# Two weight loads in one transfer each, their remainders ahead, and a bias in four transfers

## The chip, the cores and the metric

The kernel runs on one core of one Trainium2 chip. The time is the device time of an execution in microseconds (us); a median is given with its number of runs. The profiles come from single executions. Their span is from the first to the last instruction of the core, about 1.8 us shorter than the time. Ratios are computed as the mean time of one kernel's fast runs over that of the other's of the same rounds, so they are not quite the ratio of the medians quoted.

## The reference

Two tokens pass through a layer norm; then an attention over the last 2,048 keys of a cache and a squared-ReLU MLP run side by side, and both are added to the input.

```
q   = xn @ wq                          # wq: 576 x 4096
o   = softmax(q k^T / sqrt(128)) v     # 16 KV heads, 32 query heads
h   = relu(xn @ w1 + b1) ** 2          # w1: 576 x 4608
out = x + o @ wo + (h @ w2 + b2)
```

Keys, values and weights are 53 MB of bfloat16 that have to be loaded once. There is next to no arithmetic per byte.

## The kernel before

Keys and values come in 16 transfers of 2 MB (one 16,384 B row per partition) into six buffers. A packet is what one of the 16 DMA engines moves at once; in the records of this kernel that is one row of a partition, or a write of 4 B that tells a semaphore that an engine's share has landed. A semaphore is a counter on which an instruction can wait. wq and w1 have 576 = 4 x 128 + 64 rows. The first 512 come in two transfers, two rows to a partition each; the last 64, the remainder, in a third behind them:

```python
wbig = ctx.enter_context(tc.tile_pool(name="wbig", bufs=NFULL // RW))   # NFULL = 4, RW = 2
...
if i < NFULL // RW:
    tl = wbig.tile([P, RW * WBW], BF16, tag="wbig", name=f"{name}_{i}")
    rows = wt[0:NFULL * P, :].rearrange("(p r) n -> p (r n)", r=NFULL)
    nc.sync.dma_start(out=tl[:, 0:RW * width], in_=rows[:, i * RW * width:(i + 1) * RW * width])
    ...
else:
    tl = wrem.tile([P, WRW], BF16, tag="wrem", name=f"{name}_rem")
    nc.sync.dma_start(out=tl[:, 0:lrem], in_=wt[NFULL * P:D, :].rearrange("r (s l) -> (r s) l", s=S))
```

The large loads are issued on SP (SyncE), the small ones (input, biases, a few w2 rows) on ACT (ScalarE). All of them take eight semaphores in turn: a load waits until the one eight before it has landed. That is not written in the kernel. It is in the built program, and it changes whenever a load is added or removed. The matmuls of q use the four large rows first and the remainder last, and those of the MLP do the same with w1. The last w2 rows reuse w1's buffer.

## Time and profile before

| | before |
|---|---|
| time, median | 134.68 us (3 runs, 134.59 to 134.82) |
| span | 132.8 us |
| TensorE, VectorE, ScalarE busy | 66%, 43%, 35% |
| loads busy, slices 2 to 38 of 40 | 90% or more |
| packets of the SP loads | 4,320 |

How to read it: no compute engine is near its limit, and the DMA engines are busy from the first load to the last. The prediction below shows the lines and works from them. A queue's line holds packets, MB and share of the 16 engines' span. A line of the timeline holds start and length in us, engine (SPq is SP's own sequence of issues), line of the program, operation, and tile <- source; in brackets stand the idle time of the engine before it and what ended it.

### The profile page before, as it was taken

The page shows a single profiled execution, that of the slowest core. Times are in us where ns is not written, and L with a number is a line of the kernel's source. Part 1 is how long each engine was busy: PE and PEld are TensorE (multiplying, and loading weights), DVE is VectorE, ACT ScalarE, POOL GpSimd, SP SyncE. Part 2 cuts the span into 40 slices and gives each one's busy share as a digit, 9 for nine tenths or more (in the row PEclk, how much of TensorE's full clock was granted, in tenths as well). Part 3 has the DMA queues.
Part 4 walks back from the last instruction along what each step waited for, and adds up shares of the span by engine and source line. Part 5 has one row for each costly group of instructions (what it writes and reads, how often), then busy time and mean ns, then how long its engine had stood idle before and what let it go on. Part 6 is the DMA issues. An engine that isn't in the chain of part 4 may idle for free.

```text
span 132.8 us, 2335 instructions
## 1 busy us (share of the span) xinstructions
PE 87.0 (66%) x982; PEld 53.4 (40%) x982; DVE 57.4 (43%) x156; ACT 46.8 (35%) x64; POOL 5.2 (4%) x17
## 2 busy tenths in 40 slices
PE   0069737997678597397496499779725495647261
PEld 0058414375335354264264346536412154137150
DVE  7724404235465466366377437457520424350000
ACT  5715503167383276265265244366120400000000
POOL 6000000010100000100100100010100000000000
PEclk9999995559999999999999757999985555555955
DMA  4999999999999999999999999999999999999960
GB/s 124 423 414 439 419 432 434 429 424 436 410 454 423 439 419 426 422 424 434 422 434 429 429 434 442 429 433 416 433 417 440 434 421 433 427 413 431 405 239 1
DMA packets 4507, 53.76 MB, mean 405 GB/s; under 512 B 535, under 2 KB 762, under 8 KB 1278
## 3 DMA queue, kind: packets, MB, share of 16 engines
q1 hardware_dynamic: 4320, 53.32, 94.7%
q10 hardware_dynamic: 178, 0.31, 0.6%
q8 instruction: 7, 0.11, 0.3%
q14 instruction: 2, 0.02, 0.0%
HBM read 53.62 MB, written 0.00 MB: 404 GB/s over the span
## 4 chain that ended last, share of the span: by engine, by line
DMA 77%; PE 13%; SPq 4%; DVE 2%; issue 1%; ACT 0%; DVEq 0%
DMA w_rem<-in_B_w_dram 28%; DMA w<-in_B_w_dram 20%; DMA k<-in_A_k_cache_dram 17%; DMA wq_rem<-in_A_wq_dram 13%; PE kT_ps L109 8%; PE sc_ps L106 3%; SPq L134 2%; DVE qrow L292 1%; SPq L127 1%; PE o_ps L106 1%; PE qT_ps L109 1%; DVE kT L328 1%; PE out_ps L106 1%; DVE qz L308 0%; SPq L158 0%
## 5 line engine op out<-in xcount | busy, mean ns | idle before, releaser
L109 PE MATMUL kT_ps<-ident_f,k 128*128 128x128 f32 x256 | 41.9, 311 | 11.5 <-DMA k<-in_A_k_cache_dram 8.2
L109 PEld LDWEIGHTS kT_ps<-ident_f,k 128*128 128x128 f32 x256 | 32.5, 159 | 26.1 <-issue 13.2
L326 ACT COPY kT<-kT_ps 128x1024 bf16<-128x1024 bf16 x32 | 31.9, 1013 | 19.4 <-PE kT_ps L109 19.3
L328 DVE COPY kT<-kT_ps 128x1024 bf16<-128x1024 bf16 x32 | 21.8, 682 | 15.2 <-PE kT_ps L109 15.0
L106 PE MATMUL sc_ps<-kT,qz 128*32 128x512 bf16 x128 | 10.5, 413 | 5.8 <-DVE kT L328 5.8
L358 ACT ACTIVATE p<-sc_ps,bias 128x512 bf16<-128x512 f32 x8 | 5.5, 687 | 20.2 <-DVE gown L354 20.2
L106 PE MATMUL o_ps<-v,pT 128*32 128x512 bf16 x128 | 12.1, 475 | 0.0
L572 ACT CAST fin_sb<-out_ps 113x144 bf16<-113x144 f32 x1 | 0.3, 278 | 24.6 <-PE out_ps L106 24.6
L347 DVE TENSOR_REDUCE m<-sc_ps 128x1 f32<-128x512 f32 x8 | 5.5, 691 | 7.2 <-PE sc_ps L106 7.2
L387 DVE SCALAR_TENSOR_TENSOR o<-o_ps,in_s,o 128x128 f32<-128x128 f32 x24 | 8.3, 346 | 0.5
L361 DVE STREAM_TRANSPOSE pT<-p 128x512 bf16<-128x512 bf16 x8 | 5.7, 710 | 6.5 <-ACT p L358 6.5
L106 PE MATMUL out_ps<-w,hT_sb 128*17 128x144 bf16 x136 | 4.6, 295 | 4.4 <-DMA w<-in_B_w_dram 4.2
L385 DVE TENSOR_SCALAR o<-o_ps,in_s 128x128 f32<-128x128 f32 x8 | 2.7, 343 | 9.6 <-PE o_ps L106 9.6
L106 PEld LDWEIGHTS <-hT_sb 128*17 128x17 bf16 (+2 forms) x172 | 4.6, 117 | 5.7 <-issue 5.7
L106 PEld LDWEIGHTS <-xnT 128*2 128x2 bf16 x100 | 2.4, 94 | 10.8 <-issue 9.7
L351 POOL PARTITION_ALL_REDUCE gmax<-m x8 | 2.9, 365 | 90.3 <-DVE m L349 90.3
L106 PEld LDWEIGHTS <-qz 128*32 128x32 bf16 x128 | 2.2, 98 | 10.0 <-DVE kT L328 7.4
L106 PE MATMUL op_ps<-o,of_h 128*128 128x129 f32 x16 | 4.0, 334 | 3.2 <-DVE o L387 3.2
L106 PE MATMUL h_ps<-w,xnT 128*2 128x384 bf16 x48 | 3.2, 422 | 4.1 <-DMA w<-in_B_w_dram 4.1
L109 PE MATMUL pro_ps<-ident,tmp_x 2*128 2x2 bf16 x6 | 0.5, 175 | 6.6 <-DVE tmp_x L232 6.6
L106 PEld LDWEIGHTS op_ps<-o,of_h 128*128 128x128 f32 x16 | 2.8, 220 | 5.0 <-DVE o L387 5.0
L452 DVE TENSOR_TENSOR hrow<-t 98x384 bf16<-98x384 f32 x3 | 1.6, 556 | 6.5 <-ACT t L451 6.3
(74 smaller groups left out, 55.1 us busy)
## 6 DMA issues: line engine op xcount, KB each, us to landing
k<-in_A_k_cache_dram SPq DMA_DIRECT2D x8, 2048.0 KB, 12.0
v<-in_A_v_cache_dram SPq DMA_DIRECT2D x8, 2048.0 KB, 23.7
wo<-in_A_wo_dram SPq DMA_DIRECT2D x2, 2304.0 KB, 27.4
w<-in_B_w_dram SPq DMA_DIRECT2D x2, 2304.0 KB
wq<-in_A_wq_dram SPq DMA_DIRECT2D x2, 2048.0 KB, 16.6
w<-in_B_w_dram SPq DMA_DIRECT2D x3, 1296.0 KB, 27.6
w_rem<-in_B_w_dram SPq DMA_DIRECT2D x1, 576.0 KB
w<-in_B_w_dram SPq DMA_DIRECT2D x1, 576.0 KB
```

The lines of the kernel that those rows point to most:

```text
L106: tc.keep_in_program_order(nc.tensor.matmul(*a, **k))
L109: tc.keep_in_program_order(nc.tensor.transpose(*a, **k))
L134: nc.sync.dma_start(out=tl[:, 0:RW * width], in_=rows[:, i * RW * width:(i + 1) * RW * width])
L326: nc.scalar.copy(out=kT, in_=kT_ps[:])
L328: nc.vector.tensor_copy(out=kT, in_=kT_ps[:])
L347: nc.vector.tensor_reduce(out=m1[:], in_=sc_ps[:], axis=AX.X, op=ALU.max)
L351: nc.gpsimd.partition_all_reduce(gmax[:], m2[:], channels=P, reduce_op=ReduceOp.max)
L358: nc.scalar.activation(out=p_sb[:], in_=sc_ps[:], func=ACT.Exp, bias=bias[:, 0:1], scale=scale, accum_out=o1[:, Dh:Dh + 1])
L361: nc.vector.transpose(out=pT[:].rearrange("p j r -> p (j r)"), in_=p_sb[:])
L385: nc.vector.tensor_scalar(scalar1=in_s[:, 0:1], scalar2=None, op0=ALU.mult, **kw)
L387: nc.vector.scalar_tensor_tensor(scalar=in_s[:, k:k + 1], in1=o1[:, 0:Dh], op0=ALU.mult, op1=ALU.add, **kw)
L452: nc.vector.tensor_tensor(out=hrow[:, k * HB:(k + 1) * HB], in0=t1, in1=t1, op=ALU.mult)
```

## The change

The intent is fewer and larger packets: four rows of a partition in one piece (32,768 B for wq, 36,864 B for w1), with the small remainder ahead. The first MLP bias goes the other way, from one transfer of four rows to four transfers of one row.

```diff
-    wbig = ctx.enter_context(tc.tile_pool(name="wbig", bufs=NFULL // RW))
+    wbig = ctx.enter_context(tc.tile_pool(name="wbig", bufs=1))
...
-        if i < NFULL // RW:
-            tl = wbig.tile([P, RW * WBW], BF16, tag="wbig", name=f"{name}_{i}")
-            rows = wt[0:NFULL * P, :].rearrange("(p r) n -> p (r n)", r=NFULL)
-            nc.sync.dma_start(out=tl[:, 0:RW * width], in_=rows[:, i * RW * width:(i + 1) * RW * width])
+        if i == 1:
+            tl = wbig.tile([P, NFULL * WBW], BF16, tag="wbig", name=f"{name}_big")
+            nc.sync.dma_start(out=tl[:, 0:NFULL * width],
+                              in_=wt[0:NFULL * P, :].rearrange("(p r) n -> p (r n)", r=NFULL))
...
-    NW = NFULL // RW + 1
+    NW = 2
...
-    nc.scalar.dma_start(out=b1_sb[:], in_=B_b1.rearrange("(g n) -> g n", g=NG4))
+    b1_rows = B_b1.rearrange("(g n) -> g n", g=NG4)
+    for i in range(0, NG4, NG4 // 4):
+        nc.scalar.dma_start(out=b1_sb[i:i + NG4 // 4, :], in_=b1_rows[i:i + NG4 // 4, :])
```

## The prediction

> **What bounds the kernel now.** I read the slices of the span first, because a kernel that loads 53 MB for two tokens is likely to be bound by its loads, then the DMA queues, then the chain of waits, and last the issues and the matmuls around the two weight loads that change. Slices, queues and the chain's shares by engine, from the page of the kernel before:
>
> ```profile
> DMA  4999999999999999999999999999999999999960
> GB/s 124 423 414 439 419 432 434 429 424 436 410 454 423 439 419 426 422 424 434 422 434 429 429 434 442 429 433 416 433 417 440 434 421 433 427 413 431 405 239 1
> ...
> q1 hardware_dynamic: 4320, 53.32, 94.7%
> q10 hardware_dynamic: 178, 0.31, 0.6%
> q8 instruction: 7, 0.11, 0.3%
> ...
> DMA 77%; PE 13%; SPq 4%; DVE 2%; issue 1%; ACT 0%; DVEq 0%
> ```
>
> The 16 DMA engines are 90% busy or more in every slice of 3.32 us but the first and the last two, at 405 to 454 GB/s. 94.7% + 0.6% + 0.3% of 132.8 us is 126.9 us, and from the first load packet (2.2 us) to the last (129.2 us) there are 127.0 us. So there is no hole to fill. The packet records say it more sharply: on the engine that finishes first, the completions of consecutive 2 MB transfers lie at 28.19, 33.06, 37.92 and 42.78 us, 4.86 us apart. That is 131,072 B per engine in 4.86 us, 27.0 GB/s, times 16 engines 431 GB/s.
>
> The end of the chain, in order of time (start, length, what):
>
> ```profile
> 65.68 36.87 DMA w_rem<-in_B_w_dram
> 102.55 0.02 issue
> 102.56 26.58 DMA w<-in_B_w_dram
> 129.14 0.04 issue
> 129.18 0.69 PE out_ps L106 x10
> 129.88 0.02 issue
> 129.90 0.28 ACT fin_sb L572
> ```
>
> The last w2 rows land, ten matmuls, one cast, then the output store: 3.6 us of tail after the last byte. The piece "w_rem 36.87" is not a slow transfer, it is one that stood in line. The end is therefore: start of the loads + bytes over rate + tail.
>
> **What the Trainium skill says.** All three places are in the page "DMA: Bandwidth & Descriptors". Section "Where 436 GB/s comes from" gives the ceiling of the 16 ports as 435 GB/s; the trace agrees, 431 GB/s steady. Section "Why small descriptors are slow (HBM only)" names a fixed cost of about 3 cycles per packet. The records agree that it is small: consecutive packets of one engine start 47 ns apart at 1,152 B, 89 at 2,304 B, 174 at 4,608 B, 607 at 16,384 B and 682 at 18,432 B. A line of 0.0367 ns per byte plus 5 ns fits all five. Section "Why a DMA increments its semaphore by 16 and not by 1" says that the number of engines is the largest factor up to 16 of the slowest dimension, taken from the lowest-numbered engine. The trace agrees: the bias load of 4 rows left four packets of 2,304 B, at 17.90 to 17.95 us, each with one semaphore write; a load of one row leaves one.
>
> **The change part by part.**
>
> *Packets.* 4,320 packets on the load queue are 3,840 rows and 30 transfers x 16 semaphore writes. One row of a partition is one packet up to 18,432 B, the largest here. The change makes wq 128 packets of 32,768 B instead of 256 of 16,384 B, and w1 128 of 36,864 B instead of 256 of 18,432 B; the bytes stay. That removes 16 row packets and 2 semaphore writes per engine, about 5 ns each: 18 x 5 = 0.09 us. By the line a packet takes 1,208 and 1,358 ns; that it holds beyond 18,432 B is an estimate of mine. If the hardware splits such rows, the gain is 0.
>
> *First bias.* Four loads of one row instead of one of four put all four packets on the lowest engine: 3 x (89 + 6) = 0.28 us more there, 0.1 us less on the next three. The engines do not end together: their last w2 packets end at 126.81, 127.05, 127.06 and 127.33 us on four of them and between 128.17 and 129.21 us on the other twelve; the last decides. Following completions from transfer to transfer (5 engines carry the 5-partition w2 remainders, 2 the input rows, 1 the second bias), I find the lowest engine ending near 128.4 us and the slowest as one of the next three; where two completions lie within 10 ns this following is uncertain. So the added 0.28 us ends at 128.7 us, hidden, and the slowest may gain 0.1 us. Issuing four instead of one costs ACT 3 x 0.26 us near 14.3 us, where it idles until 20.95 us.
>
> *wq in one piece.* The matmuls of q as they stand:
>
> ```profile
> 14.86 1.03 PE L106 MATMUL q_ps<-wq,xnT 128*2 128x512 bf16 x16
> 18.66 1.03 PE L106 MATMUL q_ps<-wq,xnT 128*2 128x512 bf16 x16 [2.77 <-DMA wq<-in_A_wq_dram]
> 19.91 0.99 PE L106 MATMUL q_ps<-wq_rem,xnT 128*2 128x512 bf16 x8 [0.21 <-DMA wq_rem<-in_A_wq_dram]
> ```
>
> The same bytes have landed at about 19.9 us in either order, but then 40 matmuls remain instead of 8: 2 x 1.03 = 2.1 us later for q, for the first scores and for the k buffers that they free. Does that starve the loads? The issue of k after the second unit's transposes stands at 33.62 us and its bytes move only from 50.4 us; 2.1 us out of 16.8. TensorE then waits for k at 35.57, 45.60 and 55.86 us (0.41, 0.61 and 2.17 us), which swallows the delay by the fifth unit.
>
> *Waits of the issuing queue.* The two builds differ in which earlier load each issue waits for, because the loads take eight semaphores in turn and the number of loads changes. The issues of before:
>
> ```profile
> 8.43 0.55 SPq L127 DMA_DIRECT2D k<-in_A_k_cache_dram  x1
> 9.02 0.60 SPq L127 DMA_DIRECT2D v<-in_A_v_cache_dram  x1
> 10.96 0.54 SPq L127 DMA_DIRECT2D k<-in_A_k_cache_dram  x1
> 18.64 0.53 SPq L127 DMA_DIRECT2D v<-in_A_v_cache_dram  x1
> ```
>
> After it, the second k waits for the wq remainder (about 9.4 us), and the first v for the whole of wq (about 19.5 us); the next ones follow at once. While v waits, one k transfer (4.86 us) is still to move. Issue to first packet took 1.5 us at the start (0.72 to 2.19 us); the engines' spread at that point is 0.9 us. 4.86 - 0.9 - 1.5 leaves 2.5 us: no hole, but it is the thinnest place. ACT's own bias loads wait for the first k (landed 8.1 us) and for w2 pieces, all done by 14 us.
>
> *w1 in one piece.* The MLP and the last matmuls:
>
> ```profile
> 95.98 1.15 PE L106 MATMUL h_ps<-w,xnT 128*2 128x384 bf16 x24
> 101.21 2.09 PE L106 MATMUL h_ps<-w,xnT 128*2 128x384 bf16 x24 [4.08 <-DMA w<-in_B_w_dram]
> 103.09 1.18 PE L106 MATMUL h_ps<-w_rem,xnT 128*2 128x384 bf16 x12
> ...
> 120.88 1.29 PE L106 MATMUL out_ps<-w,hT_sb 128*17 128x144 bf16 x36
> 123.98 0.74 PE L106 MATMUL out_ps<-w,hT_sb 128*17 128x144 bf16 x36 [1.81 <-DMA w<-in_B_w_dram]
> 127.08 2.77 PE L106 MATMUL out_ps<-w,hT_sb 128*17 128x144 bf16 x64 [2.37 <-DMA w<-in_B_w_dram]
> ```
>
> All 60 matmuls now start at about 102.3 us. At the slow rate of the second line (2.09 us for 24) they take 5.2 us and end at 107.5 us instead of 104.3: up to 3.2 us later. Behind them TensorE has 1.81 + 2.37 = 4.2 us of waiting for w2 before the last piece, so the delay dies there with 1 us to spare. The last w2 pieces reuse w1's buffer, now one buffer, so their issue moves from the first half's matmuls to behind all of the large w1 part: about 107 us, while their bytes move from 123 us on.
>
> *Sum.* -0.09 us for packets, 0 to -0.1 us for the bias, 0 for the order: 134.68 - 0.15, about 134.5 us.
>
> **Rivals.** (1) The lowest engine is the slowest after all: +0.28 - 0.09 us, 134.9 us; for it speaks only the uncertain following of engines. (2) The MLP's delay exceeds the 4.2 us, because the granted clock falls further there: each us beyond adds 1 us, 135 to 136 us; against it, the estimate already uses the slow rate. (3) A hole at the first v: up to 1 us, 135.5 us. (4) Large packets run at another rate: the two loads take 20 of the 127 us, so 5% either way is 1 us; nothing in the line bends at 18,432 B. (5) The 7 instruction fetches of 16 KB (about 0.95 us each) fall on other engines; the slowest engine moves by some tenths either way.
>
> **Range and chances.** The sum and rivals 1 and 5 lie within 0.5 us; 134.0 to 135.0 us holds most of it. A change by 2% is 2.7 us: it needs rival 2 or 4 at a size nothing suggests.
>
> **What would show it.** Load packets fall from 4,320 to 4,320 - 256 - 32 = 4,032. The DMA slices stay at 9 and the last w2 lands at 129.0 us within 0.5. The q matmuls all stand after 19 us, the MLP's after 102 us, and the waits for w2 shrink from 4.2 us to about 1 us without vanishing. I am wrong if a slice shows under 9 before the end, if the last output matmuls no longer wait for w2, or if the large packets leave the line.

## The result, and the profile after

The changed kernel takes 134.47 us (median of 6 fast runs, 134.31 to 134.48); the kernel before took 134.63 us in its 6 runs by then (134.57 to 134.82). The ratio is 0.9984, with a 95% interval of 0.9971 to 0.9997: the same at 2%, and 0.16 us faster by the medians. The interval leaves a gain between 0.04 and 0.39 us.

Slices and queues, from the page of the changed kernel:

```profile
DMA  4999999999999999999999999999999999999960
GB/s 139 409 415 488 425 397 416 430 430 415 444 418 431 433 420 427 431 430 430 418 440 420 440 430 432 421 457 432 478 405 388 425 425 450 407 423 428 416 247 1
...
q1 hardware_dynamic: 4032, 53.32, 94.6%
q10 hardware_dynamic: 178, 0.31, 0.6%
```

The row of nines is unbroken, and the packets fell by 288 to the predicted 4,032. The single slices of 488 and 388 GB/s are no change of speed: a packet is now up to 1.36 us long and is counted in one of the 3.3 us slices. For the same reason a second profile of the same kernel shows one slice of 8 near 100 us, although by its packet records no engine stood idle there. The issues on SP at the start, from the timeline:

```profile
9.50 0.55 SPq L126 DMA_DIRECT2D k<-in_A_k_cache_dram  x1
19.80 0.54 SPq L126 DMA_DIRECT2D v<-in_A_v_cache_dram  x1
20.38 0.60 SPq L126 DMA_DIRECT2D k<-in_A_k_cache_dram  x1
```

SP now stands still from 10.1 to 19.8 us, until the large wq load has landed. No slice shows a hole, because the k transfer issued at 9.50 us was still in line. The matmuls of q:

```profile
19.82 3.58 PE L105 MATMUL q_ps<-wq_big,xnT 128*2 128x512 bf16 x32 [5.02 <-DMA wq_big<-in_A_wq_dram]
23.19 0.87 PE L105 MATMUL q_ps<-wq_rem,xnT 128*2 128x512 bf16 x8
```

q is done at 24.06 us instead of 20.90, 3.2 us later; by 56 us, where TensorE waits 1.68 us for k, it is back where it was (56.06 against 55.86 us). The MLP and the last matmuls:

```profile
102.52 3.64 PE L105 MATMUL h_ps<-w_big,xnT 128*2 128x384 bf16 x48 [7.89 <-DMA w_big<-in_B_w_dram]
105.98 0.66 PE L105 MATMUL h_ps<-w_rem,xnT 128*2 128x384 bf16 x12
...
123.57 2.37 PE L105 MATMUL out_ps<-w,hT_sb 128*17 128x144 bf16 x72
127.00 0.74 PE L105 MATMUL out_ps<-w,hT_sb 128*17 128x144 bf16 x36 [1.06 <-DMA w<-in_B_w_dram]
128.39 0.43 PE L105 MATMUL out_ps<-w,hT_sb 128*17 128x144 bf16 x16 [0.65 <-DMA w<-in_B_w_dram]
129.10 0.66 PE L105 MATMUL out_ps<-w,hT_sb 128*17 128x144 bf16 x12 [0.28 <-DMA w<-in_B_w_dram]
```

The MLP ends at 106.64 us instead of 104.27, and the waits for w2, 1.81 + 2.37 us before, are now 1.06 + 0.65 + 0.28 = 2.0 us. They shrank but did not vanish: the loads still set the end. By the packet records the last load ends at 129.13 us against 129.21.

Where do the 0.16 us come from? The profiled spans differ by 0.17 us (132.81 and 132.64 us). 0.08 us of it is the last packet's end. The rest lies behind it, and 0.07 us of that was in nobody's sum: from the landing of the output store to the end of the program it is 1.24 us before and 1.17 us after. In the built program SP closes with five instructions that each wait for a pair of the semaphores, in a fixed order; each costs about 60 ns (53 to 70 ns by the table in the experiments). The store's semaphore is in the fourth of them before, so one more follows after it has landed. The change adds one load in sum, the turn moves on by one, and the store's semaphore falls into the fifth, the last one.

### The profile page after: what moved, and what is told of

It reads as the page before. It is cut to its first block, busy times and chain, and to the rows that moved or that the text cites. A ratio compares the mean times of both kernels' runs of the same rounds, so it can differ in the third digit from the quotient of the medians.

```text
span 132.6 us, 2337 instructions
## 1 busy us (share of the span) xinstructions
PE 84.1 (63%) x982; PEld 52.2 (39%) x982; DVE 57.2 (43%) x156; ACT 46.7 (35%) x64; POOL 5.2 (4%) x17
## 2 busy tenths in 40 slices
DMA packets 4219, 53.76 MB, mean 405 GB/s; under 512 B 503, under 2 KB 730, under 8 KB 1246
## 3 DMA queue, kind: packets, MB, share of 16 engines
q1 hardware_dynamic: 4032, 53.32, 94.6%
## 4 chain that ended last, share of the span: by engine, by line
DMA 62%; PE 4%; DVE 1%; ACT 1%; issue 1%; ACTq 0%
DMA v<-in_A_v_cache_dram 29%; DMA w<-in_B_w_dram 17%; DMA k<-in_A_k_cache_dram 16%; PE kT_ps L108 3%; PE o_ps L105 1%; ACT kT L325 1%; PE sc_ps L105 1%; ACT p L357 1%; DVE pT L360 1%; DVE kT L327 0%; DVE o L386 0%; PE out_ps L105 0%; ACT fin_sb L573 0%; DVE o L384 0%; PE op_ps L105 0%
## 5 line engine op out<-in xcount | busy, mean ns | idle before, releaser
L108 PE MATMUL kT_ps<-ident_f,k 128*128 128x128 f32 x256 | 40.0, 303 | 9.3 <-DMA k<-in_A_k_cache_dram 7.0
L108 PEld LDWEIGHTS kT_ps<-ident_f,k 128*128 128x128 f32 x256 | 31.5, 155 | 22.6 <-issue 11.6
L105 PE MATMUL o_ps<-v,pT 128*32 128x512 bf16 x128 | 11.6, 461 | 0.0
L105 PEld LDWEIGHTS <-xnT 128*2 128x2 bf16 x100 | 3.1, 112 | 17.7 <-issue 17.5
L105 PE MATMUL h_ps<-w_big,xnT 128*2 128x384 bf16 x48 | 3.6, 484 | 7.9 <-DMA w_big<-in_B_w_dram 7.9
L105 PE MATMUL q_ps<-wq_big,xnT 128*2 128x512 bf16 x32 | 3.6, 625 | 5.0 <-DMA wq_big<-in_A_wq_dram 5.0
L105 PEld LDWEIGHTS <-qz 128*32 128x32 bf16 x128 | 2.2, 96 | 10.1 <-DVE kT L327 7.5
L105 PE MATMUL out_ps<-w,hT_sb 128*17 128x144 bf16 x136 | 4.1, 279 | 2.1 <-DMA w<-in_B_w_dram 2.0
L450 ACT ACTIVATE t<-h_ps 98x384 f32<-98x384 f32 x3 | 1.4, 489 | 11.0 <-PE h_ps L105 10.7
```

The lines of the kernel that those rows point to most:

```text
L105: tc.keep_in_program_order(nc.tensor.matmul(*a, **k))
L108: tc.keep_in_program_order(nc.tensor.transpose(*a, **k))
L450: nc.scalar.activation(out=t1, in_=mlp["ps"][k][0:RB, :], func=ACT.Relu)
```

## The experiments

My theory: the bytes at 5 ns per packet set the time, everything on TensorE is hidden, and the rest is at most the bias and the closing waits. Rivals: the large packets have an effect of their own; the order of the loads is nothing or everything; a packet costs nothing. Twelve kernels ran, in three calls of four; every profiled run is fast (within 1.5% of the fastest run of its kernel). The kernel before had a median of 134.71, 134.74 and 134.74 us with the three calls.

### Each part alone, and the order

Only the bias in four transfers, on the kernel before:

```diff
-    nc.scalar.dma_start(out=b1_sb[:], in_=B_b1.rearrange("(g n) -> g n", g=NG4))
+    for i in range(0, NG4, NG4 // 4):
+        nc.scalar.dma_start(out=b1_sb[i:i + NG4 // 4, :], in_=b1_rows[i:i + NG4 // 4, :])
```

> Kernel before with the first MLP bias in four one-row loads and nothing else. My theory: the four packets of 2,304 B stand on one engine, 3 x 95 ns = 0.28 us more there, hidden behind the slowest engine, which may gain 0.1 us: 134.55 to 134.70 us, ratio 0.9990 to 1.0005. Rival (the bias is the cause of the measured gain, or the lowest engine is the slowest): 134.45 us or 134.9 us.

134.67 us (6 runs), ratio 0.9994 (0.9971 to 1.0017): within my range.

Only the weight loads, with the bias in one load:

```diff
-    for i in range(0, NG4, NG4 // 4):
-        nc.scalar.dma_start(out=b1_sb[i:i + NG4 // 4, :], in_=b1_rows[i:i + NG4 // 4, :])
+    nc.scalar.dma_start(out=b1_sb[:], in_=B_b1.rearrange("(g n) -> g n", g=NG4))
```

> Changed kernel with the bias in one load again. My theory: 16 row packets and 2 semaphore writes fewer per engine at 5 ns each, -0.09 us: about 134.55 us, ratio 0.9993. Rival (all of the gain comes from the large packets): ratio 0.9984. Rival (none does): 1.0000. The three differ by less than the spread of single runs, so the packet records decide: 1,213 and 1,364 ns for the large packets, 4,032 packets.

134.79 us (134.67 to 134.98), ratio 1.0002. The packets are as expected, 1,213 and 1,364 ns long and 4,032 in number, but the time is slower than each of the three expectations, and not one of its six runs is as fast as the slowest of the changed kernel's control (below). Both parts alone are no faster than the kernel before, and together they are. That made me look behind the last load, where the closing waits show:

```
kernel                        closing waits behind the store's   store landed to end
before                        1                                  1.24 us
changed / its control         0                                  1.17 / 1.16 us
bias alone                    3                                  1.33 us
weights alone                 3                                  1.35 us
remainders last               0                                  1.17 us
```

So 0.11 us of the weights-only run's time against before, and 0.09 us of the bias-only run's, are the turn of the semaphores and not the loads. Against the control (134.38 us) the weights-only run is 0.41 us slower; the turn accounts for 0.19 us of that, and the cause of the rest was not found. At an equal turn (134.54 us, below) 0.07 to 0.16 us are left.

The remainders behind the large loads again, otherwise the changed kernel:

```diff
-        if i == 1:
+        if i == 0:
             tl = wbig.tile([P, NFULL * WBW], BF16, tag="wbig", name=f"{name}_big")
```

> Changed kernel with the remainders behind the large weight loads instead of ahead. My theory: the second k then waits for the large wq load (landed 18.0 us, issue 18.6 us, first packet about 1.5 us later, 20.1 us), while only the remainder, done at 18.5 to 19.3 us, is left to move: a hole of 0.8 us on the late engines and 1.6 us on the early ones, and the end moves by 0.8 us: about 135.2 us, ratio 1.004. Rival (the order does nothing, the bytes are the same): 134.5 us, ratio 0.998.

135.70 us (135.65 to 135.83), ratio 1.0071. Slices of that run and its issues at the place:

```profile
DMA  4999968999999999999999999999899999999960
GB/s 148 420 439 442 451 248 353 455 406 441 408 451 415 441 411 442 424 421 446 414 436 416 446 416 446 426 452 490 386 402 415 431 431 445 420 415 418 431 270 1
```

```profile
8.26 0.33 SPq L138 DMA_DIRECT2D wq_rem<-in_A_wq_dram  x1
18.35 0.54 SPq L126 DMA_DIRECT2D k<-in_A_k_cache_dram  x1
```

The sixth and seventh slices fall to 248 and 353 GB/s: the second k waits for the large wq load, and by then only the remainder is left in line. The packet records show the 16 engines idle for 1.05 us each on average between 18 and 26 us, and for nothing before that. The engines were done with the remainder at 18.25 to 19.56 us, and the first packets of k started at 19.68 to 19.98 us, 1.3 to 1.6 us after the issue. I had put the hole at 0.8 us on the late engines and 1.6 us on the early ones, and the end at the late ones' 0.8. The end moved by 1.2 to 1.3 us, half a us more than expected; the last load ends 1.03 to 1.18 us later than in the two profiles of the changed kernel, which is about the mean hole. So "remainders ahead" is not decoration: with four rows in one transfer it is what keeps a load in line while SP waits.

The changed kernel once more:

> The changed kernel once more, as the control of this call. Ratio 0.9984 as measured before, within 0.001; 134.4 to 134.5 us.

134.38 us (134.24 to 134.59), ratio 0.9974 (0.9951 to 0.9998), as expected within the spread. Of the eleven runs of the kernel before in this call one (135.67 us), and in the third call another (136.03 us), lies about 1 us above the others and counts as fast. They lower the ratios of these calls: without its own, this one is about 0.9979.

### The same semaphores in turn

To compare weights alone with the changed kernel at the same turn, three loads of 64 B stand in for the three missing bias loads:

```diff
+    tiny_sb = const.tile([3, 32], BF16, name="tiny_sb")
+    for i in range(3):
+        nc.scalar.dma_start(out=tiny_sb[i:i + 1, :], in_=B_b1[0:32].rearrange("(o n) -> o n", o=1))
```

> The run with the whole weight loads and one bias load, plus three loads of 64 B on the lowest engine, so that the loads take the same semaphores in turn as in the changed kernel and the output store's semaphore is again the last one waited for. My theory: the closing waits cost 65 ns each and three of them stood behind the store in that run, none here: 134.79 - 0.19 = 134.6 us, with 1.16 us from the store's landing to the end instead of 1.35; what is left against the changed kernel (0.1 to 0.2 us) is the bias on four engines. Rival (the closing waits are nothing, the bias is all): 134.8 us.

135.38 us: a miss, and by the rival as well. The last load ends at 130.07 us. There is no hole, but three of the sizes have longer packets by their medians: 613 ns instead of 611 at 16,384 B, 688 instead of 686 at 18,432 B, 1,366 instead of 1,364 at 36,864 B. Those of 4,096, 10,368 and 32,768 B stay at 159, 389 and 1,213 ns. In the built program the new tile of 64 B stands ahead of all k, v and weight tiles, which until then began on 512 B boundaries; now each begins 64 B behind one. Two runs test that. First the same three loads into a padding tile that the kernel has anyway, so that nothing moves:

```diff
-    const.tile([P, 96], F32, name="pad_0")
+    pad_0 = const.tile([P, 96], F32, name="pad_0")
...
+    tiny_sb = pad_0[:].bitcast(BF16)
+    for i in range(3):
+        nc.scalar.dma_start(out=tiny_sb[i:i + 1, 0:32], in_=B_b1[0:32].rearrange("(o n) -> o n", o=1))
```

> The whole weight loads, one bias load and three loads of 64 B again, but the 64 B land in a padding tile that is there anyway, so every other tile stands at the address it has in the changed kernel. My theory for the surprise of the run before (135.4 us): its small tile moved all later tiles by 64 B off a 512 B boundary, and every packet took 2 to 3 ns more. So here 134.5 to 134.65 us, packets of 16,384 B back at 611 ns, 1.16 us from the store's landing to the end. Rival (the small loads themselves cost it): 135.4 us again.

134.54 us (134.53 to 134.57, 5 runs), 611 ns, and 1.15 us from store to end: as expected. Then the shift alone, on the changed kernel:

```diff
+    const.tile([P, 16], F32, name="pad_2")     # 64 B, used by nothing
```

> The changed kernel with a 64 B tile that nothing uses ahead of the k and v tiles, and no other edit: same loads, same waits. My theory: all large tiles stand 64 B off a 512 B boundary, packets of 16,384 B take 613 ns, the last load lands 0.6 to 0.9 us later: 135.0 to 135.3 us, ratio 1.003 to 1.005. Rival (placement is nothing): 134.45 us, ratio 0.998.

135.26 us (135.20 to 135.40), 613 ns, the last load at 129.95 us. An unused tile of 64 B costs 0.8 us, five times what the change gains. That the placement costs it is shown; the small loads are cleared. How it does so is not. The median hides the spread: in the changed kernel 1,890 of 2,048 packets of 16,384 B took 611 ns; here 564 did, and the others mostly 612 to 620. Added up over the load queue, the packets take 0.50 to 0.54 us more per engine, while the last load ends 0.82 and 0.68 us later than in the two profiles of the changed kernel. Why the 32,768 B packets into the same buffer keep their length stays open too.

Against this, the bias in one load at equal turn and placement (134.54 us) and in four (134.38 and 134.47 us, of other calls) differ by 0.07 to 0.16 us. The prediction had up to 0.1 us, the first run with the 64 B loads 0.1 to 0.2. Over the kernel before of their own rounds they are 0.9977 (about 0.9987 without the outlying run) against 0.9984 and 0.9974 (0.9979): no effect of the bias's four loads is established.

### What a packet costs

> Changed kernel with every k and v load written as four pieces of 4,096 B per partition in the same 16 transfers. My theory: 384 row packets more per engine at 4.3 to 5 ns each, +1.65 to +1.9 us: 136.1 to 136.4 us, ratio 1.012 to 1.014, 10,176 load packets. Rival (the cost of a packet hides behind its neighbours, or the hardware joins the pieces): 134.5 us.

```diff
-        return [lambda i=i: nc.sync.dma_start(out=tl[:, i * n:(i + 1) * n], in_=v[:, :, i * n:(i + 1) * n])
+        return [lambda i=i: nc.sync.dma_start(
+            out=tl[:, i * n:(i + 1) * n].rearrange("p (a m) -> p a m", m=n // 4),
+            in_=v[:, :, i * n:(i + 1) * n].rearrange("c h (a m) -> c h a m", m=n // 4))
```

134.51 us, but the test was void. The page of that run has

```profile
q1 hardware_dynamic: 4032, 53.32, 94.6%
```

and the built program has rows of 8,192 elements again: pieces that touch were joined before they got to the chip. The next run keeps the pieces 128 B apart in the tile, in the two wo loads:

```diff
-        tl = wopool.tile([P, WR, D], BF16, tag="wo_sb", name=f"wo_{t}")
+        tl = wopool.tile([P, WR, D + 64], BF16, tag="wo_sb", name=f"wo_{t}")[:, :, 0:D]
```

> The changed kernel with the 16 rows of wo in each partition 128 B apart in the tile, so that a load can't be joined to one packet: 1,152 B packets instead of 18,432 B ones in the two wo loads. My theory of 5 ns per packet: 16 x 47.2 ns = 755 ns instead of 682 ns per partition, 8 partitions per engine, 2 loads: +1.16 us, 135.6 us, ratio 1.007 (4,032 + 3,840 = 7,872 load packets). Rival (a packet's cost hides behind its neighbours): 134.45 us.

135.68 us (135.66 to 135.72), ratio 1.0061. The whole page counts the added packets among those under 2 KB:

```profile
DMA packets 8059, 53.76 MB, mean 401 GB/s; under 512 B 503, under 2 KB 4826, under 8 KB 5342
```

8,059 against 4,219 in the changed kernel are 3,840 more, 240 per engine. Against the 134.38 to 134.47 us of the changed kernel this is 1.21 to 1.30 us, 5.0 to 5.4 ns per packet. The rows lie 1,280 B apart, so half of them are 256 B off a 512 B boundary; but 4,076 of the 4,096 packets took the same 51 ns, so placement is not what this run pays for. A packet's cost did not hide here, where the engines are never idle. Turned around, the 16 row packets that the change removes per engine are worth 0.08 us, and the two semaphore writes a hundredth more.

### The slack on TensorE

> Changed kernel with the large w1 load moved behind one v load of 2 MB: w1 lands 4.86 us later, so the MLP starts 4.86 us later and everything behind it on TensorE too. In the changed kernel TensorE still waits 1.06 + 0.65 + 0.28 = 2.0 us for w2. My theory: the delay uses up the 2.0 us and the rest shows: +2.6 to +2.9 us, 137.0 to 137.3 us, ratio 1.018 to 1.021, and no wait for w2 any more. Rival (the loads alone set the end, the order of equal bytes is nothing): 134.5 us.

```diff
-            for i in range(NW):
-                issue_w1(i)
+            issue_w1(0)
         if u == 5:
-            for v in (NU - 2, NU - 1):
-                load_v(v)
+            load_v(NU - 2)
+            issue_w1(1)
+            load_v(NU - 1)
```

136.95 us (136.56 to 137.34), ratio 1.0162, just under my range. The MLP starts at 107.25 us instead of 102.52, 4.7 us later. The last output matmuls, from the timeline of that run:

```profile
126.67 2.10 PE L105 MATMUL out_ps<-wo,ws 128*17 128x144 bf16 x64 [1.55 <-DVE ws L419]
128.56 3.68 PE L105 MATMUL out_ps<-w,hT_sb 128*17 128x144 bf16 x136
```

All 136 matmuls on w2 run in one go, with no wait for a load, and the loads are done at 129.00 us, 0.13 us earlier than in the changed kernel. The bytes are the same; 4.7 us of delay used up 2.0 us of slack, and most of what was left came out at the end.

### Which engine is last

> As the last one, but one of the small loads is 29 rows of 2,304 B, which all fall on one engine: 29 x 89.5 ns = 2.6 us more work there. My theory (engine followed to an end near 128.4 us, slowest at 129.2): 128.4 + 2.6 = 131.0 us for the last load, +1.8 us: 136.4 us, ratio 1.013. Rival (the lowest engine is the slowest): +2.6 us, 137.2 us. Rival (it is one of the four that end at 127.0 us): +0.5 us, 135.1 us. Rival (engines share the work): +0.16 us.

```diff
+    low_sb = const.tile([29, 1152], BF16, name="low_sb")
+    nc.scalar.dma_start(out=low_sb[:], in_=B_w2[0:58, :].rearrange("(a b) n -> a (b n)", b=2))
+    # and two of the 64 B loads
```

140.65 us, ratio 1.0434, far outside each expectation. Its slices show why it answers another question:

```profile
DMA  4999999996099999999999999999998999999960
GB/s 152 405 459 408 444 406 433 419 428 273 18 354 429 434 411 423 425 439 411 434 436 411 425 448 415 437 412 495 393 467 349 444 420 435 420 414 430 414 231 1
```

Between 33.2 and 38.9 us the engines stand idle for 4.5 us each on average. The load is small (67 KB) but all on one engine, whose two queues take turns packet by packet: its packets come almost all singly, one per 16,384 B packet of the other queue, 0.70 us apart. So its last row starts at 36.6 us, 22 us after the issue, and SP's v load, eight behind it in the turn, waits for it (us in total, times, longest us):

```profile
SPq L126 <- DMA low_sb<-in_B_w_dram: 15.9, 1, 15.9
```

The large tiles are moved in this run too, to 320 B behind a 512 B boundary in the built program, and its 16,384 B packets have the same median of 613 ns. Which engine is last stays open here.

The w2 remainders over all 16 engines instead of five:

```diff
-    XS = ((8, 20, 5), (1, 96, 96))
+    XS = ((8, 16, 16), (1, 128, 128))
+    # and three 64 B loads into pad_0 that keep the turn
```

> The changed kernel with the w2 remainders loaded over all 16 engines (16 partitions of 8 rows, 128 of 1 row) instead of on the lowest five, and three 64 B loads into the padding tile so that the turn of the semaphores stays. My theory: the lowest five engines have 0.93 us less to do, the other eleven 0.46 us more; the ones with an instruction fetch, which ended from 128.24 us on, become the last at 128.7 to 129.0 us, so the last load lands 0.1 to 0.4 us earlier: 134.1 to 134.35 us, ratio 0.995 to 0.997. Rival (the engines even out by themselves, or the last one isn't among the lowest five): 134.45 to 134.9 us.

135.54 us (134.98 to 135.76), ratio 1.0048: a miss. The engines do end closer together (128.41 to 130.34 us, 1.9 us apart instead of 2.3), but all of them later. The time goes at the start: the first k lands at 9.2 to 9.6 us instead of 7.5 to 7.9, and

```profile
GB/s 123 313 326 493 402 471 393 421 441 416 436 424 431 431 431 431 421 441 426 429 421 441 421 441 426 440 402 490 430 435 375 455 406 452 418 410 425 424 255 1
```

the second and third slices run at 313 and 326 GB/s. The 9,216 B packets of these rows took up to 984 ns there instead of 347. What slowed the reads is not settled, so this run says nothing firm about the last engine either. No experiment beat the changed kernel.

## Why the prediction was right

- **The bound.** Right. In twelve of the thirteen other profiles the loads are the end, and the one where they are not (w1 behind v) had been made so.
- **Packets, -0.09 us.** The count is exact. Start to start the large packets take 1,209 and 1,360 ns against 1,208 and 1,358 on the line; two of half the size take 2 x 607 = 1,214 and 2 x 682 = 1,364 ns, so the records show 5 and 4 ns saved by each. The cost per packet, 5 ns from spacings, is confirmed by an experiment that adds 240 of them (5.0 to 5.4 ns). The saving itself is smaller than the spread between two profiles' last packets (129.13 and 129.27 us for the same kernel), so its 0.09 us rests on these packet times and isn't seen in the end time.
- **Bias, 0 to -0.1 us.** The four packets stood on one engine as predicted, at 17.99, 19.30, 20.61 and 21.92 us. That they cost no time is measured (134.38 and 134.47 us with four loads, 134.54 with one, at an equal turn); that the lowest engine was not the last rests on the following of completions alone, since the packet records do not name the engine and both tests of it failed.
- **wq in one piece.** Mechanism right, one term mis-sized: q came 3.2 us later, not 2.1. The 40 matmuls took 4.2 us in all at a granted clock of 0.53, against 1.00 at the place I had taken the 1.03 us from. It was hidden all the same. One reading was off without consequence: the bytes of the k issued at 33.62 us began to move at 47.6 us on the first engine and at 50.0 us on the last, so the room was 14 us and not 16.8.
- **Waits of the issuing queue.** Right to 0.3 us in the first profile (9.50 and 19.80 us for 9.4 and 19.5), to 0.7 us in the control's (10.06 and 19.73 us), and no hole. The run with the remainders last shows what the place costs when no k is in line: 1.2 to 1.3 us.
- **w1 in one piece.** Right in kind, and on the safe side in size: the MLP ended at 106.6 us, not 107.5, and 2.0 us of waiting for w2 were left instead of 1. Delaying it further cost time as soon as the slack was gone.
- **What the sum lacked.** "0 for the order" left out the end of the program: 0.07 us of the gain come from the output store's semaphore being the last one waited for. The total was right partly because 0.09 and 0.07 make 0.16; I had filled that place with part of a bias effect that no run establishes. That the forecast met the time to 0.03 us was luck in this part, and the spread of the runs does not separate the two terms in the time itself.

## What to carry to other kernels

When the load engines are never idle, count bytes and packets before anything else, and ask of each reordering only two things: whether a load stays in line while the queue waits, and whether the compute behind the last load still has slack. When a change is worth tenths of a microsecond, compare kernels only at equal addresses of the large tiles and at an equal turn of the semaphores: a tile of 64 B cost 0.8 us here, and three loads more or fewer moved the end by 0.1 to 0.2 us.

## What the Trainium skill lacked or had wrong

- Tile addresses. "DMA: Bandwidth & Descriptors", section "How a descriptor splits into AXI transactions", says that a descriptor that does not start 256B-aligned pays for the bytes before its start. It speaks of what is fetched, and gives no figure for large rows. Here the place to which the rows are written moved: 64 B off a 512 B boundary made most of the 16,384 B packets 1 to 9 ns longer, and the kernel 0.8 us slower (135.26 us against 134.47).
- Packets taking turns. The same page, section "Queues, rings and completion order", has the engines take turns between queues packet by packet, with typically about 9 to 17 descriptors to a packet. The runs agree on the turns, but not on that number: 29 rows of one load came almost all singly, 0.70 us apart, each behind one row of the other queue, and four bias loads 1.31 us apart beside rows of 1.21 us. The page doesn't warn how late a small load then lands (22 us after its issue).
- No page that I read has the waits on the loads' semaphores with which the kernel's own program closes: about 60 ns each, 1.15 to 1.35 us from the output store's landing to the end.
- No page that I read says that touching pieces of a transfer are joined when the program is built: 4,032 packets where I had written pieces for 10,176.
